# Sliding-window attention and a SiLU feed-forward: batch 1's q and k turned two positions at once, a margin on landings in the planned order, shorter fillers, one weight piece moved

## The chip, the cores and the metric

The kernel runs on one core of one Trainium2 chip. A core has five engines that run side by side: TensorE (PE; its weight loads are shown apart as PEld), VectorE (DVE), ScalarE (ACT), GpSimd (POOL) and SyncE (SP). POOL and SP also issue DMAs. The metric is the device time of one execution in microseconds (us); lower is better. A kernel's time is the median of several runs.

## What is computed

Eight batches of eight heads, 576 positions, head size 64. Each position attends to itself and the 63 before it. The result, 4608 rows of 512, goes through a feed-forward layer with SiLU.

```python
scores = scale * np.matmul(q, k.transpose(0, 1, 3, 2))
mask = (rel >= 0) & (rel < 64)
scores = np.where(mask, scores, -1000000000.0)
attn = softmax(scores)
x = np.matmul(attn, v)  # [8, 8, 576, 64] to [4608, 512]
h = x @ w_in            # [512, 2048]
out = (h * sigmoid(h)) @ w_out   # [2048, 512]
```

## The kernel before

**Order.** Nothing is scheduled by the framework. A class `Plan` writes the order by hand: every piece of work is put in with the engines that may do it, a cost in us, what it depends on, and a rank. `Plan.run` then plays a clock forward in a small model of its own. Whenever an engine is free it takes the ready piece of lowest rank, and in the end the pieces are emitted in that order. On the chip each engine goes through its list in order and waits at an instruction whose inputs are not there, with all that stands behind it. The model's times are thus only used to choose the order. For a DMA, `op["seen"]` is when the model believes that it has landed.

**Loads.** q, k, v, w_in and w_out come in through POOL's queue, cast to bf16 on the way. Only the first q and k go through SP. POOL issues in this order: q1, k1, then the constants `ident` and `window` (memsets and selects on POOL itself), then q2, q3, k2, k3 and the four v parts of batch 0 (`FIRST_LOADS`), eight pieces of w_in, and batch 1. Batch 1 has a q and a k load for each of four head pairs `pj` (here called positions) into the tiles `natb`, with v parts 0 and 1 after pair 1 and parts 2 and 3 after pair 3. Then come eight pieces of w_out, and batch 2.

**Turns.** q and k are needed with the head dimension on the partitions, so `natb` is turned on TensorE by a matmul with the identity `ident`, into a PSUM bank. `natb` holds 96 partitions with six positions side by side for each of two heads. `turn_heads` takes one position of one head at a time: 12 matmuls for a pair (line 315), then one copy, `lift` (line 340), into `qt` or `kt`. `turn_twos` takes two positions of a head side by side: 6 matmuls (line 324). The even positions then lie on partitions 0 to 63 and the odd ones on 64 to 127, and four copies, `lift_twos` (line 333), carry out one head and one parity each. Before, batch 1's q and k use `turn_heads`, the q of batches 2 and 3 use `turn_twos`, and the rest is transposed by DMA (line 268). Batch 0 has a form of its own (`turn_first`, line 303).

**Attention.** A batch has three groups of three 64-position blocks. For batches 0 and 1 a group is two units, one for pairs 0 and 1 and one for 2 and 3. A unit is: scores (line 365), exp on ACT (379), mask on DVE (382), values (388), reciprocal and scaling on DVE (395, 401), a turn back on PE (405) and the copy into `bridge` (416).

**Feed-forward.** Nine tiles of 512 rows. First layer: 16 groups of four matmuls of 512 columns (line 421), each followed by SiLU on ACT (427). Second layer: 64 matmuls (line 430), copied out and stored by SP. Tile 0's first layer runs while batch 1 is loaded and turned; its second layer shares TensorE with batch 1's attention. Tile 1's first layer needs all of batch 1's `bridge`.

**PSUM.** Eight banks: four called `at` (turns and scores) and four called `mp` (feed-forward, values of later batches).

**Fillers.** Up to 60 matmuls of `ident` (line 685, class "warm", lowest rank) are put in wherever TensorE would stand idle in the model, until the first feed-forward matmul is placed.

Of the kernel before, what the change touches and what calls it, by code (L numbers as in the profile page):

```python
# [14 lines left out]
class Plan:  # L15
# [35 lines left out]
    def run(self):  # L51
# [7 lines left out]
        while left:  # L59
# [6 lines left out]
            while moved:  # L66
                moved = False
                for e in engines:
                    if free[e] > now:
                        continue  # L70
                    best, kept = None, set()
                    heads = [(self.queues[c][head[c]], c) for c in can[e] if head[c] < len(self.queues[c])]
                    for op, c in sorted(heads, key=lambda x: x[0]["first"]):
                        if e == "POOL" and op["dma"] and len(sent) >= 8 and sent[-8] > now:
                            continue
                        if e not in op["us"] or not self.done(op["deps"]) or (op["gate"] and not op["gate"]()):
                            continue
# [12 lines left out]
                        break  # L90
                    if best is None:
                        continue
                    op, c = best
                    head[c] += 1
                    us = op["us"][e]
                    if op["table"] and op["table"] != table:
                        table, us = op["table"], us + 1.28
                    end = free[e] = now + us
                    soft = e == "POOL"
                    if op["dma"] is None:  # L100
                        op["seen"] = end + op["lat"]
# [25 lines left out]
def kernel(ctx, tc, q, k, v, w_in, w_out, out):  # L127
    nc = tc.nc
# [165 lines left out]
    def at_bf16(op, i=0):  # L294
        return banks[op["bank"][i]].bitcast(BF16)[:, 0:S]
# [10 lines left out]
                        is_transpose=True, start=(m == 0), stop=(m == NM0 - 1),  # L306
                    )

    def turn_heads(op, w):

        pst = at_bf16(op).rearrange("x (m p) -> x m p", m=NM)
        heads = natbs[w][0:NR].rearrange("p (h m d) -> p h m d", h=2, m=NM)
        for m in range(NM):
            for hh in range(2):
                nc.tensor.matmul(
                    pst[64 * hh:64 * hh + 64, m], lhsT=heads[:, hh, m], rhs=ident[0:NR, 0:NR],
                    is_transpose=True, start=(m == 0), stop=(m == NM - 1),
                )

    def turn_twos(op, w):  # L320

        pst = at_bf16(op).rearrange("x (m p) -> x m p", m=NM)
# [6 lines left out]
    def place_one(b, pj, kk):  # L329
        return kt[b % NK][:, 64 + pj * S:64 + (pj + 1) * S] if kk else qt[b % NK][:, pj * S:(pj + 1) * S]  # L330

    def lift_twos(e, op, b, pj, hh, r):
        copies[e](  # L333
            out=place_one(b, pj, 0)[64 * hh:64 * hh + 64].rearrange("x (p m) -> x p m", m=NM)[:, :, r::2],
            in_=at_bf16(op)[64 * r:64 * r + 64].rearrange("x (h m p) -> x h p m", h=2, m=NM // 2)[:, hh],
        )

    def lift(e, op, b, pj, kk, i=0):
        m = NM if b else NM0
        copies[e](  # L340
            out=place_one(b, pj, kk).rearrange("x (p m) -> x p m", m=m),
            in_=at_bf16(op, i).rearrange("x (m p) -> x p m", m=m),
        )

    def shift_v(e, b, hf, a, z):
# [119 lines left out]
    def late(b):  # L465
        return hold.get(b)

    def add_first_batch():
        got = {}
        for what, u in FIRST_LOADS:  # L470
# [21 lines left out]
            for i in range(2):  # L492
                x = 2 * a + i
                tu["untils"][i].append(p.add("lift", {"ACT": 0.64, "DVE": 0.75}, lambda e, tu=tu, x=x, kk=kk, i=i:
                                             lift(e, tu, 0, x, kk, i), [tu, c_k[0]]))
                kq_done[(0, x)] = kq_done.get((0, x), []) + tu["untils"][i]
            for w in ws:
                natb_free[w] = tu

    def add_batch_qk(b):  # L500
        pool = "at" if b else "all"
        slot, parts = {}, {0: [], 1: []}
        for pj in range(NP):
            kq_done[(b, pj)] = []
        for pj in range(NP):
            busy = s_last.get((b - NK, pj), []) + ([c_k[b % NK]] if b < NK else [])
            for kk in range(2):
                if b >= (NXK if kk else NXQ):
                    if pj % 2 == 0:
# [1 line left out]
                        n_nat[0] += 1  # L511
                    i = slot[kk]
                    parts[kk] += [p.add("dma", {"POOL": 0.72}, lambda _, i=i, pj=pj, kk=kk, hh=hh: load_rows(i, b, pj, kk, hh),
                                        [nat_free.get(i)], dma=0.5, gate=late(b)) for hh in range(2)]
# [7 lines left out]
                    for x in (pj - 1, pj):  # L522
# [2 lines left out]
                w = n_nat[1] % NNB  # L525
                n_nat[1] += 1
                ca = [p.add("dma", {"POOL": 0.66}, lambda _, w=w, pj=pj, kk=kk: load_cast(w, b, pj, kk),
                            [natb_free.get(w)], dma=0.65, gate=late(b))]
                twos = b > 1 and not kk
                tu = p.add("turn", {"PE": 0.27 if twos else 0.5}, None, ca + [c_ident], lat=0.1, pool=pool, b=b)  # L530
                tu["fn"] = lambda _, tu=tu, w=w, twos=twos: (turn_twos if twos else turn_heads)(tu, w)
                li = []
                if twos:
                    for hh, r in [(0, 0), (0, 1), (1, 0), (1, 1)]:
                        li.append(p.add("lift", {"ACT": 0.48, "DVE": 0.48}, lambda e, tu=tu, pj=pj, hh=hh, r=r:
                                        lift_twos(e, tu, b, pj, hh, r), [tu] + busy + li, b=b))
                else:
                    li.append(p.add("lift", {"ACT": 0.64, "DVE": 0.75}, lambda e, tu=tu, pj=pj, kk=kk:
                                    lift(e, tu, b, pj, kk), [tu] + busy, b=b))
                tu["untils"][0] = li  # L540
                natb_free[w] = tu
                kq_done[(b, pj)] += li
            if b < NIV and pj % 2:
                add_v_loads(b, [pj - 1, pj], [c_vv[b]])

    def add_v_loads(b, parts, busy):
        v_landed.setdefault(b, []).extend(
            p.add("dma", {"POOL": 1.0}, lambda e, part=part: load_v(e, b, part), busy, dma=1.1, gate=late(b)) for part in parts)

    def add_batch_v(b):  # L550
        busy = pv_last.get(b - NV, []) + [c_vv[b % NV]]
# [189 lines left out]
```

## Time and profile before

| what | us |
|---|---|
| median of 7 runs | 310.39 (308.93 to 315.34) |
| the profiled execution | 308.93, span 307.2 |
| PE busy, whole span | 296.6 |
| first matmul of the feed-forward (line 421) starts | 19.83 |
| batch 1's turns (line 315) | 26.36 to 34.28 |
| first second-layer matmul (line 430) | 39.38 |
| tile 1's first layer starts | 59.55 |
| POOL's last loads are issued | about 160 |

The span in 40 slices (7.7 us each; busy tenths):

```profile
PE   5999999999999999999999999999999999999995
DVE  2671447433653057304650266005500000000000
ACT  4887777678548665667456745773574146216611
POOL 8957759869697586852860000000000000000000
DMA  7999999999999999999999949303310110010011
```

A digit 9 means 90% or more. TensorE is full from the second slice on; the DMA engines are full for the first 60% of the span, while the inputs come in. The time from a load's issue to its landing is read from its semaphore: the landings named in this document are those times in the trace.

### The profile page before, as it was taken

The page shows a single profiled execution, that of the slowest core. Times are in us where ns is not written, and L with a number is a line of the kernel's source. Part 1 is how long each engine was busy: PE and PEld are TensorE (multiplying, and loading weights), DVE is VectorE, ACT ScalarE, POOL GpSimd, SP SyncE. Part 2 cuts the span into 40 slices and gives each one's busy share as a digit, 9 for nine tenths or more (in the row PEclk, how much of TensorE's full clock was granted, in tenths as well). Part 3 has the DMA queues.
Part 4 walks back from the last instruction along what each step waited for, and adds up shares of the span by engine and source line. Part 5 has one row for each costly group of instructions (what it writes and reads, how often), then busy time and mean ns, then how long its engine had stood idle before and what let it go on. Part 6 is the DMA issues. An engine that isn't in the chain of part 4 may idle for free.

```text
span 307.2 us, 6690 instructions
## 1 busy us (share of the span) xinstructions
PE 296.6 (97%) x2704; PEld 148.1 (48%) x2733; DVE 93.8 (31%) x256; ACT 180.4 (59%) x331; POOL 118.6 (39%) x159
## 2 busy tenths in 40 slices
PE   5999999999999999999999999999999999999995
PEld 3575445444554445445544454444544444444444
DVE  2671447433653057304650266005500000000000
ACT  4887777678548665667456745773574146216611
POOL 8957759869697586852860000000000000000000
PEclk9999999999999999999999999999999999999999
DMA  7999999999999999999999949303310110010011
GB/s 156 172 196 184 184 199 161 126 236 173 161 175 149 156 162 162 175 166 138 195 147 176 109 128 198 69 2 93 98 25 2 68 68 1 36 68 34 2 68 68
DMA packets 137598, 37.56 MB, mean 122 GB/s; under 512 B 122464, under 2 KB 132832, under 8 KB 137568
## 3 DMA queue, kind: packets, MB, share of 16 engines
q0 software_dynamic: 95328, 18.06, 76.0%
q1 hardware_dynamic: 42240, 19.08, 32.9%
q8 instruction: 21, 0.34, 0.4%
q14 instruction: 9, 0.07, 0.1%
HBM read 36.70 MB, written 9.44 MB: 150 GB/s over the span
## 4 chain that ended last, share of the span: by engine, by line
PE 87%; DMA 6%; POOL 5%; issue 2%; ACT 0%; POOLq 0%; ACTq 0%
PE mp L430 41%; PE mp L421 38%; DMA w_in_sb<-in_moe_w_in_dram 4%; PE at L365 3%; PE mp L388 3%; DMA natb<-in_k_dram 2%; POOL w_in_sb L282 2%; POOL vv L276 1%; POOL natb L249 1%; PE at L324 1%; PE at L388 1%; PE at L405 0%; POOL natb L243 0%; PE mp L405 0%; ACT g L427 0%
## 5 line engine op out<-in xcount | busy, mean ns | idle before, releaser
L430 PE MATMUL mp<-w_out_sb,g 128*128 128x512 bf16 (+2 forms) x579 | 128.7, 368 | 2.9 <-issue 2.1
L421 PE MATMUL mp<-bridge,w_in_sb 128*128 128x512 bf16 (+2 forms) x600 | 129.6, 370 | 0.2 <-ACT g L427 0.2
L427 ACT ACTIVATE g<-mp 128x512 bf16<-128x512 f32 (+2 forms) x150 | 85.6, 580 | 32.4 <-PE mp L421 31.6
L421 PEld LDWEIGHTS <-w_in_sb 128*128 128x128 bf16 x600 | 57.4, 97 | 66.7 <-issue 6.3
L430 PEld LDWEIGHTS <-g 128*128 128x128 bf16 x608 | 55.6, 98 | 58.5 <-issue 0.2
L379 ACT ACTIVATE e<-at 128x384 bf16<-128x384 f32 x90 | 37.8, 497 | 23.1 <-PE at L365 22.7
L436 ACT COPY ot<-mp 128x512 f32<-128x512 f32 (+2 forms) x31 | 17.2, 558 | 57.4 <-PE mp L430 39.5
L262 POOL DMA_DIRECT2D nat<-in_k_dram x48 | 35.9, 753 | 19.5 <-DMA vv<-in_v_dram 10.1
L382 DVE TENSOR_TENSOR e<-e,mask 128x384 bf16<-128x384 bf16 x84 | 27.0, 352 | 46.4 <-ACT e L379 45.8
L276 POOL DMA_DIRECT2D vv<-in_v_dram x32 | 32.4, 1022 | 6.5 <-PE mp L421 2.3
L262 POOL DMA_DIRECT2D nat<-in_q_dram x32 | 24.3, 767 | 6.3 <-DMA nat<-in_q_dram 3.7
L401 DVE TENSOR_TENSOR ox<-mp,rc 128x384 bf16<-128x384 f32 x39 | 19.3, 534 | 0.0
L388 PEld LDWEIGHTS <-e 128*64 128x64 bf16 x576 | 11.5, 110 | 10.9 <-issue 9.5
L395 DVE RECIPROCAL rc<-mp 128x6 f32<-128x6 f32 x39 | 7.3, 192 | 21.7 <-PE mp L388 21.7
L365 PEld LDWEIGHTS <-kt 64*128 64x128 bf16 x576 | 10.0, 95 | 6.3 <-issue 5.5
L365 PE MATMUL at<-qt,kt 64*128 64x64 bf16 x540 | 12.4, 191 | 0.0
L436 DVE COPY ot<-mp 128x512 f32<-128x512 f32 x7 | 4.7, 690 | 24.0 <-PE mp L430 23.7
L333 DVE COPY qt<-at 64x288 bf16<-64x288 bf16 x18 | 8.6, 479 | 8.8 <-ACT qt L333 5.6
L388 PE MATMUL mp<-vv,e 128*64 128x65 bf16 x468 | 11.2, 196 | 0.0
L350 DVE COPY vv<-vv 64x576 bf16<-64x576 bf16 (+1 forms) x13 | 7.7, 592 | 7.1 <-issue 3.6
L243 POOL DMA_DIRECT2D natb<-in_q_dram x12 | 7.9, 655 | 4.5 <-DMA w_out_sb<-in_moe_w_out_dram 1.1
L348 DVE COPY vv<-vv 64x576 bf16<-64x576 bf16 (+1 forms) x13 | 8.5, 651 | 0.2
(63 smaller groups left out, 123.7 us busy)
## 6 DMA issues: line engine op xcount, KB each, us to landing
out_dram<-ot SPq DMA_DIRECT2D x35, 256.0 KB, 2.6
vv<-in_v_dram POOLq DMA_DIRECT2D x32, 144.0 KB, 7.0
nat<-in_k_dram POOLq DMA_DIRECT2D x48, 72.0 KB, 7.5
nat<-in_q_dram POOLq DMA_DIRECT2D x32, 72.0 KB, 7.9
natb<-in_q_dram POOLq DMA_DIRECT2D x15, 144.0 KB, 6.7
w_in_sb<-in_moe_w_in_dram POOLq DMA_DIRECT2D x8, 256.0 KB, 8.0
w_out_sb<-in_moe_w_out_dram POOLq DMA_DIRECT2D x8, 256.0 KB, 7.4
natb<-in_k_dram POOLq DMA_DIRECT2D x7, 144.0 KB, 5.9
```

What stands on the lines that cost most here:

```text
L262: nc.gpsimd.dma_start(out=rows(i)[:, pj % 2, :, 64 * hh:64 * hh + 64], in_=(q, k)[kk][b, head(pj, hh)].rearrange("(m p) d -> p m d", p=NR),)
L276: queue[e].dma_start(out=vv[b % NV][:, 2 * g0 + 1:2 * g1 + 1:2, 0:D], in_=v[b].rearrange("h s d -> (h s) d").rearrange("(g p) d -> p g d", ...
L333: copies[e](out=place_one(b, pj, 0)[64 * hh:64 * hh + 64].rearrange("x (p m) -> x p m", m=NM)[:, :, r::2], in_=at_bf16(op)[64 * r:64 * r + ...
L365: nc.tensor.matmul(at_six(of[hh])[:, j, x], lhsT=kt[b % NK][r, at:at + 128], rhs=qt[b % NK][r, at:at + 64], start=(b > 0 and j == x == 0), ...
L379: nc.scalar.activation(out=es[n % NE], in_=at_six(bank), func=ACTF.Exp, scale=scale)
L382: nc.vector.tensor_mul(es[n % NE], es[n % NE], mask0 if g == 0 else mask)
L388: nc.tensor.matmul(at_pv(bank)[64 * hh:64 * hh + 64, j, x], lhsT=es[(2 * n + hh) % NE][:, j, x], rhs=vv[b % NV][:, head(2 * a + j, hh) * N ...
L401: nc.vector.tensor_mul(ox(n), at_pv(bank)[:, :, :, 0:D], rcs[n % NRC].unsqueeze(3).to_broadcast([128, 2, 3, D]))
L421: nc.tensor.matmul(banks[bank["bank"][0]][:, lo:hi], lhsT=w_in_sb[:, c, ft * 128:(ft + 1) * 128], rhs=bridge[:, (j * TT + lo) // 64:(j * T ...
L427: nc.scalar.activation(out=gts[gt][:, lo:hi], in_=banks[bank["bank"][0]][:, lo:hi], func=ACTF.Silu)
L430: nc.tensor.matmul(banks[bank["bank"][0]][:, 0:hi - lo], lhsT=gts[gt][:, m * 128:(m + 1) * 128], rhs=w_out_sb[:, f, lo:hi], start=(f == 0) ...
L436: copies[e](out=ots[ot][:, lo:hi], in_=banks[bank["bank"][0]][:, 0:hi - lo])
```

## The change

It does five things.

1. Batch 1's q and k are turned by `turn_twos` and carried out by four `lift_twos` each, to `qt` or `kt`. `turn_heads` goes, and `lift` stays for batch 0 alone.
2. In the model, the loads of later q and k, of v from batch 1 on, and of w_out count as landed 1.3 us later (`MARGIN`). The kernel on the chip has no wait for that; only the order can change.
3. Fillers end when the last exp of batch 0 is placed, not when the first feed-forward matmul is.
4. w_out's first piece (`EARLY_OUT`) is issued ahead of batch 1's v parts 2 and 3, not behind them.
5. q2 and q3 of batch 0 join q1 and k1 in the class "early", whose rank is ahead of the constants on POOL. The q turns of batch 3 take `mp` banks instead of `at`.

```diff
-                        op["seen"] = pipe[True] + (1.2 if now < 40 else 3.2)
+                        op["seen"] = pipe[True] + op["lat"] + (1.2 if now < 40 else 3.2)
...
-    FIRST = 6
+    FIRST, EARLY_OUT = 6, 1
...
-    NM0, LEAD = 9, 1.5
+    NM0, LEAD, MARGIN = 9, 1.5, 1.3
...
-    def lift_twos(e, op, b, pj, hh, r):
+    def lift_twos(e, op, b, pj, kk, hh, r):
         copies[e](
-            out=place_one(b, pj, 0)[64 * hh:64 * hh + 64].rearrange("x (p m) -> x p m", m=NM)[:, :, r::2],
+            out=place_one(b, pj, kk)[64 * hh:64 * hh + 64].rearrange("x (p m) -> x p m", m=NM)[:, :, r::2],
...
-                ca = p.add("early" if u == 1 else "dma", {"POOL": 0.6}, lambda _, w=w, u=u, kk=kk: load_first_cast(w, u, kk), dma=0.8)
+                ca = p.add("early" if (what, u) in FIRST_LOADS[2:6] else "dma", {"POOL": 0.6}, lambda _, w=w, u=u, kk=kk: load_first_cast(w, u, kk), dma=0.8)
...
+    def add_w_out(which):
+        wout.extend(p.add("dma", {"POOL": 0.75}, lambda _, f=f: load_w_out(f), dma=1.29, lat=MARGIN) for f in which)
+
     def add_batch_qk(b):
-        pool = "at" if b else "all"
+        pool = "mp" if b == 3 else "at"
...
-                            [natb_free.get(w)], dma=0.65, gate=late(b))]
-                twos = b > 1 and not kk
-                tu = p.add("turn", {"PE": 0.27 if twos else 0.5}, None, ca + [c_ident], lat=0.1, pool=pool, b=b)
-                tu["fn"] = lambda _, tu=tu, w=w, twos=twos: (turn_twos if twos else turn_heads)(tu, w)
+                            [natb_free.get(w)], dma=0.65, gate=late(b), lat=MARGIN)]
+                tu = p.add("turn", {"PE": 0.27}, None, ca + [c_ident], lat=0.1, pool=pool, b=b)
+                tu["fn"] = lambda _, tu=tu, w=w: turn_twos(tu, w)
                 li = []
-                if twos:
-                    for hh, r in [(0, 0), (0, 1), (1, 0), (1, 1)]:
...
-                else:
-                    li.append(p.add("lift", {"ACT": 0.64, "DVE": 0.75}, lambda e, tu=tu, pj=pj, kk=kk:
-                                    lift(e, tu, b, pj, kk), [tu] + busy, b=b))
+                for hh, r in [(0, 0), (0, 1), (1, 0), (1, 1)]:
+                    li.append(p.add("lift", {"ACT": 0.48, "DVE": 0.48}, lambda e, tu=tu, pj=pj, kk=kk, hh=hh, r=r:
+                                    lift_twos(e, tu, b, pj, kk, hh, r), [tu] + busy + li, b=b))
...
             if b < NIV and pj % 2:
+                if pj == 3:
+                    add_w_out(range(EARLY_OUT))
                 add_v_loads(b, [pj - 1, pj], [c_vv[b]])
...
-    p.add_filler(60, "warm", {"PE": 0.26}, warm, [c_ident], gate=lambda: moe[0][0]["seen"] is None,
+    p.add_filler(60, "warm", {"PE": 0.26}, warm, [c_ident], gate=lambda: exps[0][-1]["seen"] is None,
...
-            for f in range(8):
-                wout.append(p.add("dma", {"POOL": 0.8}, lambda _, f=f: load_w_out(f), dma=1.28))
+            add_w_out(range(EARLY_OUT, 8))
```

The row loads of k and q (`load_rows`) and the v loads from batch 1 on get `lat=MARGIN` in the same way. On each queue the new order is: POOL issues q1, k1, q2, q3, the constants, k2, k3, v and so on as before, and further down w_out piece 0 between batch 1's pair 3 and its v part 2. SP's queue is not edited.

More of the change, by code (lines that the diff above doesn't have):

```diff
@@ L307, in turn_first @@
                     )
[L309 to L318, printed above, removed]
     def turn_twos(op, w):
@@ L330, in place_one, with lift @@
         return kt[b % NK][:, 64 + pj * S:64 + (pj + 1) * S] if kk else qt[b % NK][:, pj * S:(pj + 1) * S]
-    def lift_twos(e, op, b, pj, hh, r):
+    def lift_twos(e, op, b, pj, kk, hh, r):
         copies[e](
-            out=place_one(b, pj, 0)[64 * hh:64 * hh + 64].rearrange("x (p m) -> x p m", m=NM)[:, :, r::2],
+            out=place_one(b, pj, kk)[64 * hh:64 * hh + 64].rearrange("x (p m) -> x p m", m=NM)[:, :, r::2],
             in_=at_bf16(op)[64 * r:64 * r + 64].rearrange("x (h m p) -> x h p m", h=2, m=NM // 2)[:, hh],
         )
-    def lift(e, op, b, pj, kk, i=0):
-        m = NM if b else NM0
+    def lift(e, op, pj, kk, i):
         copies[e](
-            out=place_one(b, pj, kk).rearrange("x (p m) -> x p m", m=m),
-            in_=at_bf16(op, i).rearrange("x (m p) -> x p m", m=m),
+            out=place_one(0, pj, kk).rearrange("x (p m) -> x p m", m=NM0),
+            in_=at_bf16(op, i).rearrange("x (m p) -> x p m", m=NM0),
         )
@@ L494, in add_first_batch @@
                 tu["untils"][i].append(p.add("lift", {"ACT": 0.64, "DVE": 0.75}, lambda e, tu=tu, x=x, kk=kk, i=i:
-                                             lift(e, tu, 0, x, kk, i), [tu, c_k[0]]))
+                                             lift(e, tu, x, kk, i), [tu, c_k[0]]))
                 kq_done[(0, x)] = kq_done.get((0, x), []) + tu["untils"][i]
@@ L513, in add_batch_qk @@
                     parts[kk] += [p.add("dma", {"POOL": 0.72}, lambda _, i=i, pj=pj, kk=kk, hh=hh: load_rows(i, b, pj, kk, hh),
-                                        [nat_free.get(i)], dma=0.5, gate=late(b)) for hh in range(2)]
+                                        [nat_free.get(i)], dma=0.5, gate=late(b), lat=MARGIN) for hh in range(2)]
                     if pj % 2 == 0:
@@ L527, in add_batch_qk @@
                 ca = [p.add("dma", {"POOL": 0.66}, lambda _, w=w, pj=pj, kk=kk: load_cast(w, b, pj, kk),
-                            [natb_free.get(w)], dma=0.65, gate=late(b))]
-                twos = b > 1 and not kk
-                tu = p.add("turn", {"PE": 0.27 if twos else 0.5}, None, ca + [c_ident], lat=0.1, pool=pool, b=b)
-                tu["fn"] = lambda _, tu=tu, w=w, twos=twos: (turn_twos if twos else turn_heads)(tu, w)
+                            [natb_free.get(w)], dma=0.65, gate=late(b), lat=MARGIN)]
+                tu = p.add("turn", {"PE": 0.27}, None, ca + [c_ident], lat=0.1, pool=pool, b=b)
+                tu["fn"] = lambda _, tu=tu, w=w: turn_twos(tu, w)
                 li = []
-                if twos:
-                    for hh, r in [(0, 0), (0, 1), (1, 0), (1, 1)]:
-                        li.append(p.add("lift", {"ACT": 0.48, "DVE": 0.48}, lambda e, tu=tu, pj=pj, hh=hh, r=r:
-                                        lift_twos(e, tu, b, pj, hh, r), [tu] + busy + li, b=b))
-                else:
-                    li.append(p.add("lift", {"ACT": 0.64, "DVE": 0.75}, lambda e, tu=tu, pj=pj, kk=kk:
-                                    lift(e, tu, b, pj, kk), [tu] + busy, b=b))
+                for hh, r in [(0, 0), (0, 1), (1, 0), (1, 1)]:
+                    li.append(p.add("lift", {"ACT": 0.48, "DVE": 0.48}, lambda e, tu=tu, pj=pj, kk=kk, hh=hh, r=r:
+                                    lift_twos(e, tu, b, pj, kk, hh, r), [tu] + busy + li, b=b))
                 tu["untils"][0] = li
@@ L547, in add_v_loads @@
         v_landed.setdefault(b, []).extend(
-            p.add("dma", {"POOL": 1.0}, lambda e, part=part: load_v(e, b, part), busy, dma=1.1, gate=late(b)) for part in parts)
+            p.add("dma", {"POOL": 1.0}, lambda e, part=part: load_v(e, b, part), busy, dma=1.1, gate=late(b), lat=MARGIN * (b > 0)) for part in parts)
     def add_batch_v(b):
```

## The prediction

> **What bounds the kernel now.** I read the page's busy times and chain first, then the chain in order of time, then TensorE's timeline where that chain leaves TensorE.
>
> ```profile
> PE 296.6 (97%) x2704; PEld 148.1 (48%) x2733; DVE 93.8 (31%) x256; ACT 180.4 (59%) x331; POOL 118.6 (39%) x159
> ...
> PE 87%; DMA 6%; POOL 5%; issue 2%; ACT 0%; POOLq 0%; ACTq 0%
> ```
>
> PE carries 87% of the chain. The rest is loading at the start, up to 33.9 us, as the chain in order of time shows (start, length, what):
>
> ```profile
> 27.66 6.20 DMA natb<-in_k_dram
> 33.90 0.45 PE at L315 x12
> 34.35 4.64 PE mp L421 x21
> ...
> 54.77 4.75 PE mp L430 x22
> 59.55 5.99 PE mp L421 x27
> ```
>
> The last k load of batch 1 lands at 27.66 + 6.20 = 33.86, and its turn starts at 33.90. From there PE runs to the end (304.1) with nearly no gap: between 38.9 and 59.5 it is busy 20.39 of 20.60 us. So a microsecond of PE time or PE wait saved ahead of 39 us is one off the end, if nothing behind runs late. TensorE's timeline (start, length to the modelled end, line):
>
> ```profile
> 28.27 0.39 PE L421 MATMUL mp<-bridge,w_in_sb 128*128 128x512 bf16 x1
> 28.92 0.45 PE L315 MATMUL at<-ident,natb 96*64 96x96 bf16 x12 [0.26 <-DMA natb<-in_k_dram]
> ...
> 31.77 0.45 PE L315 MATMUL at<-ident,natb 96*64 96x96 bf16 x12
> 32.15 0.39 PE L421 MATMUL mp<-bridge,w_in_sb 128*128 128x512 bf16 x1
> 32.47 0.45 PE L315 MATMUL at<-ident,natb 96*64 96x96 bf16 x12
> ...
> 33.90 0.45 PE L315 MATMUL at<-ident,natb 96*64 96x96 bf16 x12 [0.29 <-DMA natb<-in_k_dram]
> 34.28 4.71 PE L421 MATMUL mp<-bridge,w_in_sb 128*128 128x512 bf16 x21
> ```
>
> Each turn stands in PE's order just where its load lands, and where the load is late, the first-layer matmuls behind it wait too. Batches 2 and 3 already turn q two positions at once:
>
> ```profile
> 65.37 0.42 PE L324 MATMUL at<-ident,natb 96*128 96x96 bf16 x6
> 65.63 1.68 PE L421 MATMUL mp<-bridge,w_in_sb 128*128 128x512 bf16 x7
> 67.14 0.42 PE L324 MATMUL at<-ident,natb 96*128 96x96 bf16 x6
> ```
>
> **The turns.** Between 65.63 and 67.14 seven matmuls take 1.51 us, 0.216 each. A two-position turn then adds 65.63 - 65.37 = 0.26 us. A one-position turn adds 32.15 - 31.77 = 0.38, plus a slower entry: from 32.15 the next turn follows after 0.32, 0.104 over a matmul's 0.216. That is 0.48 us. The stretch from the last matmul ahead of the first turn (26.05) to 34.28 is 8.23 us and holds 16 matmuls (3.46), so eight turns and their waits cost 4.77. Eight turns at 0.48 are 3.86, the waits 0.91. With turns at 0.26 (2.08) and no wait, 4.77 - 2.08 = 2.69 us go: 1.78 from the form, 0.91 from the waits.
>
> A rule speaks against the first part. The Trainium skill, "TensorE: Matmul & The Clock Gate", section on LDWEIGHTS, says that a weight load takes the number of its columns over 1.2 GHz. By that, 12 loads of 64 columns and 6 of 128 cost the same (an estimate: 0.64 us both), and the form would save nothing; the sum would be 1.78 us smaller. The rows disagree: 109 ns for a load of 64 columns at L315, 98 for 128 at L324. I go by the rows.
>
> **The margin.** With 1.3 us added to planned landings, turns stand later in PE's order, behind about six more 0.216 us matmuls. The lateness seen was under 0.4 us a time (0.652 from matmul to turn at 28.92, against 0.32). Once PE has gained some 2.7 us against the loads, though, a turn would meet its load that much earlier, and the margin gives back only part: I keep 0.2 us of wait (bounds 0 and 0.91). After 59.5 the margin only shifts turns and scores among matmuls; I take nothing (bounds: a gain of 0.2, the idle time left between 38.9 and 59.5, and a loss of 0.5, about one more wait like today's largest). On POOL the loads keep their order, and SP's queue is not touched.
>
> **The lifts, the price of the form.** A turn was carried out of PSUM by one copy and now takes four, each waiting for the one before in the same tile (duration min/median/max):
>
> ```profile
> L340 ACT COPY kt<-at x3: 638/638/639, 27.6 to 33.0; 128x576 bf16<-128x576 bf16 x3
> L340 DVE COPY kt<-at x1: 758/758/758, 34.5 to 34.5; 128x576 bf16<-128x576 bf16 x1
> ...
> L333 DVE COPY qt<-at x18: 467/480/491, 49.1 to 74.4; 64x288 bf16<-64x288 bf16 x18
> L333 ACT COPY qt<-at x14: 466/474/479, 50.4 to 75.3; 64x288 bf16<-64x288 bf16 x14
> ```
>
> Before: 6 x 0.64 + 2 x 0.76 = 5.4 us. After: 32 x 0.48 = 15.4 us, so 10 us more for ACT and DVE. Here is what they have (length; busy us of PE, PEld, DVE, ACT, POOL):
>
> ```profile
> 26.30:38.90 12.60, 11.88 (x133) 5.83 (x132) 4.29 (x10) 9.11 (x15) 10.44 (x15) 1.00 1.64 182
> ```
>
> Free are 8.3 us of DVE and 3.5 of ACT: 11.8 for 10 more. It fits barely, and half of it comes late: the last four loads land from 31.7 to 33.9. Sixteen lifts of batch 2 took 7.7 us on both engines (49.09 to 56.82) beside attention work; from 32.2 that ends at 39.9. Batch 1's first scores need only positions 0 and 1 and can start at 38.9 - 2.7 = 36.2. The second unit needs 2 and 3; it started at 39.1, now about 40. In between PE has second-layer matmuls. The attention's last bridge then ends at 54.4 + 0.9 = 55.3, and tile 1's first layer, which needs it, starts at 59.55 - 2.7 = 56.85: covered by 1.5 us. I take 0.4 us of loss (bounds 0, and 1 us if the order places those scores before the lifts are out). A lift on ACT between two silus (busy 0.60 of each 0.87 us) delays a silu by 0.2 us; four `mp` banks, 3.5 us of matmuls, cover that.
>
> **w_out ahead of v.** w_out's first piece is issued at 28.28 in place of v part 2 and lands one piece's pace after 33.86: 1.34 (two pieces land at 38.39 and 39.73), so 35.2 instead of 36.97. It is needed by the first L430, at 36.2 + 0.45 = 36.65: without the move PE would wait 0.3. The second piece lands at 38.39 as now, and PE reaches it after eight matmuls, 36.65 + 1.73 = 38.38: level. v parts 2 and 3 land at 36.1 and 37.1 instead of 34.78 and 35.80; their DVE shifts wait, and behind them the values of unit 2, later than that anyway. Nothing, then.
>
> **q2 and q3 early.** Two issues (3.74 to 4.88, 1.14 us) move ahead of `ident` and `window` on POOL. `ident` is done at 4.2 instead of 3.05; the first turn needs it at 5.14, when ACT's cast is in. The fillers start 1.14 us later. DVE's bias waits as long, needed only at 8.8. The loads land at 6.03 (k1), then 7.90, 8.60, 9.35, 10.17: a hole of 1.1 us closes, but k2 is issued as late as now and the fastest load took 4.0 us, so what follows gains some 0.4. Batch 0's end hangs on DVE, gapless from 13.1 to 20.6, which starts on v: 0.3 us gained (bounds: 0.4, and a loss of 0.5 if late fillers slow the first turns).
>
> **Fillers end sooner.** Four run from 19.17 to 19.83 ahead of the first L421. But its input is ready only when DVE's second bridge ends, 19.11 + 0.55 = 19.66. So 0.1 us at most. **Batch 3's turns in `mp`**: a bank held some 2.7 us (65.37 to 68.07) leaves three for first-layer groups whose own round is about 1.8 us. Nothing (bounds 0 and a loss of 0.3).
>
> **Sum**: 2.69 - 0.2 - 0.4 + 0.3 + 0.1 = 2.5 us. The profiled run took 308.93 (span 307.2): 306.4. It was the fastest of the seven; the median, 310.39, lies 1.46 above, so I say 310.4 - 2.5 = 307.9. The bounds: all good 2.69 + 0.2 + 0.4 + 0.1 = 3.4, so 307.0; all bad 2.69 - 0.91 - 0.5 - 1.0 - 0.5 - 0.3 = -0.5, so 310.9.
>
> **Rivals.** *The lifts eat it.* With 10 us more ACT and DVE are 23.4 of 25.2 us taken in that stretch, so scores and silus run late and 1.5 to 2.5 us of the gain go: 309.4 to 310.4, no change. For it: that share, 93%. Against: DVE's 4.29 of 12.6 us today.
>
> *The attention of batch 1 runs out of cover (slower).* Tile 1's first layer waits once unit 2's scores start after 39.1 + (56.85 - 54.4) = 41.5. If the last sixteen lifts run on one engine at the chained pace of batch 2's first turn (DVE starts 49.09 and 49.84, 0.75 apart), they end at 34.2 + 16 x 0.75 = 46.2: 4.7 us lost against 2.7 won, 312.4. For it: the chain of four, and ACT's silus come first. Against: two chains interleave and ACT took 14 of 32 such copies.
>
> *The clock.* Fillers start at 4.24. Full rate came after 8 us: 36 turn matmuls take 0.99 us at 5.14 and 0.66 at 10.22. If it comes some 3.4 us later (5.14 to 8.6 again), at most half of that is lost, 1.7: 309.6. The Trainium skill, same page, Part 1, has the full clock follow a busy, free-running window of 3.4 us; by it a start 1.1 us later costs a whole window in about a third of the runs (an estimate). One profile cannot show it.
>
> *Only the form works*, the margin moving nothing useful: 1.8 - 0.4 + 0.4 = 1.8, 308.6. It lies inside the forecast.
>
> **Chances.** Forecast with the last case, 0.65, own range 306.4 to 308.8; lifts 0.15; clock 0.05; cover 0.15. About 0.5% (1.55 us) is what can be told from no change: faster (under 308.8) 0.65, same 0.20, slower (over 311.9) 0.15. The range reaches up through both middle cases to the edge of the slower one: 306.2 to 311.6.
>
> **What would show it.** Right: eight groups of six L324 matmuls ahead of the first L430 with no DMA releaser, the first L430 near 36.7, tile 1's first L421 near 56.9, w_out's first landing near 35. Wrong: PE waiting at L365 for DVE or ACT `kt` or `qt` near 40, at L421 for a bridge near 57, or turns of 0.99 us past 8.6.

## The result: 313.39 us, slower by 0.7%, and the profile after

The changed kernel takes 313.39 us (median of 27 runs, 309.64 to 316.89); the kernel before, on the same chips, 310.35 (64 runs, 308.49 to 315.62). The ratio is 1.0073, with a 95% interval of 1.0052 to 1.0094; it compares the fast runs alone, those within 1.5% of the fastest of their kernel, while the medians of all runs are 1.0% apart. The forecast was 307.9. The profiled execution after took 314.84 us, 1.4 above the median, span 313.1.

The steps of both profiled executions, each time the start of the first matmul of that kind (us):

| step | before | after | difference |
|---|---|---|---|
| tile 0, first layer | 19.8 | 20.0 | +0.2 |
| tile 0, second layer | 39.4 | 36.6 | -2.8 |
| tile 1, first layer | 59.5 | 59.0 | -0.5 |
| tile 2 | 92.2 | 93.3 | +1.1 |
| tile 3 | 124.7 | 125.5 | +0.7 |
| tile 4 | 156.9 | 163.5 | +6.6 |
| tile 5 | 189.1 | 194.6 | +5.5 |
| end of TensorE | 304.0 | 309.6 | +5.6 |

At 36.6 TensorE is 2.8 us ahead, but 0.7 of that is work that no longer stands ahead of this point and comes behind it. At tile 1, 0.5 is left. Then tile 3 lasts 38.0 us in place of 32.2. On the page, the lines that answer to those shown of before are the busy times, the chain and, of the 40 slices, the granted clock (before, all 40 digits are 9):

```profile
PE 296.2 (95%) x2645; PEld 147.5 (47%) x2675; DVE 102.7 (33%) x273; ACT 184.9 (59%) x340; POOL 117.5 (38%) x159
...
PEclk9999999999999999999799999999999999999999
...
PE 79%; DMA 13%; POOL 3%; issue 2%; DVE 1%; ACT 0%; SPq 0%; POOLq 0%; ACTq 0%
```

TensorE does no more work than before, but carries 79% of the chain, not 87, and DMA carries 13%. One slice, the twentieth (149 to 157 us), has a clock below full. The chain in order of time says which DMA (start, length, what):

```profile
125.64 12.23 PE mp L409 x56
...
138.36 10.66 DMA kt<-nat
149.58 4.44 PE mp L418 x12
```

At 138.36 SP issues the transpose of batch 5's last two k pairs; it lands 10.66 us later. TensorE's timeline (line 353 is the scores, 376 the values, 418 the second layer, in the changed kernel's numbers):

```profile
144.72 0.35 PE L353 MATMUL at<-qt,kt 64*128 64x64 bf16 x12
149.07 0.35 PE L353 MATMUL at<-qt,kt 64*128 64x64 bf16 x12 [4.00 <-DMA kt<-nat]
149.58 4.44 PE L418 MATMUL mp<-w_out_sb,g 128*128 128x512 bf16 x12 [0.16 <-issue]
```

The first half of batch 5's first unit runs, the second half waits 4.0 us for `kt`, and the twelve matmuls behind take 4.44 us, 0.37 each. The stretches around it (length; busy us of PE, PEld, DVE, ACT, POOL; granted clock; DMA share; GB/s) show why:

```profile
145.10:149.00 3.90, 0.00 (x0) 0.00 (x0) 1.39 (x4) 0.87 (x2) 1.02 (x2) 1.00 1.90 108
149.86:153.27 3.41, 3.41 (x10) 1.19 (x9) 0.72 (x2) 0.46 (x2) 2.25 (x4) 0.50 1.81 187
```

After 3.9 us without a matmul the clock is granted at half for 3.41 us; that is some 1.7 us of matmuls lost. Wait and clock together, 4.0 + 1.7, are the 5.8 us by which tile 3 is longer.

The times of the other executions fit this. One such half-clock stretch takes the mean granted clock of a whole execution to 0.995 (0.5 x 3.41 us of 313.1 lost), and 23 of the 28 executions of the changed kernel have 0.995 or less, with a median of 313.82 us. The five without took 309.64 to 312.00, with a median of 310.19, no slower than the kernel before.

Before, the same `kt` was issued at 136.04, landed at 146.25, and was needed at 147.8:

```profile
147.84 0.52 PE L365 MATMUL at<-qt,kt 64*128 64x64 bf16 x24
```

So it comes 2.8 us later after, but is also needed 3 us sooner; together they use up the 1.6 us to spare. Of the 2.8, 2.3 are a later issue. On SP's queue the transposes and the store ahead of this one follow one another with almost no gap, from 122.78 before and from 123.63 after, and they take 1.5 us longer in all after; why is not shown. Why it is needed sooner is seen in tile 1's second layer (matmuls of the scores between 70 and 90 us, 24 to a unit), before and after:

```profile
L365 PE MATMUL at<-qt,kt x72: 190/190/200, 76.5 to 87.3; 64*128 64x64 bf16 x72
```

```profile
L353 PE MATMUL at<-qt,kt x96: 190/190/200, 73.5 to 87.2; 64*128 64x64 bf16 x96
```

Three units of attention before, four after: from there all attention runs one unit ahead. Batch 5's first unit is the third to start in tile 3's second layer before (138.8, 144.0, 147.8), the second after (139.6, 144.7).

How the front part went. The turns and lifts of the changed kernel (line 313 is the turn of two positions, 409 the first layer, 322 the four lifts):

```profile
28.19 0.42 PE L313 MATMUL at<-ident,natb 96*128 96x96 bf16 x6
28.45 0.60 PE L409 MATMUL mp<-bridge,w_in_sb 128*128 128x512 bf16 x2
28.88 0.42 PE L313 MATMUL at<-ident,natb 96*128 96x96 bf16 x6
...
36.64 2.09 PE L418 MATMUL mp<-w_out_sb,g 128*128 128x512 bf16 x7
38.66 0.35 PE L353 MATMUL at<-qt,kt 64*128 64x64 bf16 x12
38.94 0.82 PE L418 MATMUL mp<-w_out_sb,g 128*128 128x512 bf16 x3
40.74 0.41 PE L313 MATMUL at<-ident,natb 96*128 96x96 bf16 x6 [0.98 <-DVE kt L322]
```

```profile
L322 DVE COPY kt<-at x10: 471/478/487, 29.7 to 42.3; 64x288 bf16<-64x288 bf16 x10
...
L322 ACT COPY kt<-at x6: 471/475/479, 31.3 to 43.8; 64x288 bf16<-64x288 bf16 x6
```

Each turn adds 0.26 us (28.45 - 28.19), as forecast, and none waits for its load. But seven, not eight, stand ahead of the second layer. The eighth is at 40.74 and waits 1.0 us for a lift: a bank is free only when four lifts are out, and the last of these copies starts at 43.8.

### The profile page after: what moved, and what is told of

The parts are those of the page before. It is cut to its first block, busy times and chain, and to the rows that moved or that the text cites. A ratio compares the mean times of both kernels' runs of the same rounds, so it can differ in the third digit from the quotient of the medians.

```text
span 313.1 us, 6586 instructions
## 1 busy us (share of the span) xinstructions
PE 296.2 (95%) x2645; PEld 147.5 (47%) x2675; DVE 102.7 (33%) x273; ACT 184.9 (59%) x340; POOL 117.5 (38%) x159
## 4 chain that ended last, share of the span: by engine, by line
PE 79%; DMA 13%; POOL 3%; issue 2%; DVE 1%; ACT 0%; SPq 0%; POOLq 0%; ACTq 0%
PE mp L418 37%; PE mp L409 35%; DMA kt<-nat 3%; DMA natb<-in_q_dram 3%; PE mp L376 3%; DMA w_out_sb<-in_moe_w_out_dram 3%; PE at L353 3%; DMA vv<-in_v_dram 2%; DMA nat<-in_k_dram 1%; POOL natb L249 1%; POOL w_out_sb L288 1%; POOL vv L276 1%; PE at L376 1%; POOL natb L243 0%; PE at L313 0%
## 5 line engine op out<-in xcount | busy, mean ns | idle before, releaser
L418 PE MATMUL mp<-w_out_sb,g 128*128 128x512 bf16 (+2 forms) x578 | 131.5, 371 | 2.9 <-issue 1.9
L418 PEld LDWEIGHTS <-g 128*128 128x128 bf16 x608 | 55.7, 98 | 59.0 <-issue 2.5
L367 ACT ACTIVATE e<-at 128x384 bf16<-128x384 f32 x88 | 36.8, 497 | 26.3 <-PE at L353 25.2
L424 ACT COPY ot<-mp 128x512 f32<-128x512 f32 (+2 forms) x28 | 15.4, 555 | 57.5 <-PE mp L418 44.9
L262 POOL DMA_DIRECT2D nat<-in_k_dram x48 | 35.2, 738 | 17.3 <-DMA nat<-in_k_dram 7.6
L262 POOL DMA_DIRECT2D nat<-in_q_dram x32 | 23.6, 741 | 14.1 <-DMA nat<-in_q_dram 6.5
L389 DVE TENSOR_TENSOR ox<-mp,rc 128x384 bf16<-128x384 f32 x37 | 18.5, 537 | 0.0
L383 DVE RECIPROCAL rc<-mp 128x6 f32<-128x6 f32 x37 | 7.1, 195 | 20.6 <-PE mp L376 20.5
L424 DVE COPY ot<-mp 128x512 f32<-128x512 f32 x10 | 6.8, 690 | 20.0 <-PE mp L418 18.9
L338 DVE COPY vv<-vv 64x576 bf16<-64x576 bf16 (+1 forms) x14 | 8.7, 624 | 5.9 <-DMA vv<-in_v_dram 5.6
L322 DVE COPY qt<-at 64x288 bf16<-64x288 bf16 x16 | 7.7, 479 | 7.5 <-ACT qt L322 7.1
## 6 DMA issues: line engine op xcount, KB each, us to landing
vv<-in_v_dram POOLq DMA_DIRECT2D x32, 144.0 KB, 8.2
natb<-in_q_dram POOLq DMA_DIRECT2D x15, 144.0 KB, 6.3
natb<-in_k_dram POOLq DMA_DIRECT2D x7, 144.0 KB, 5.5
```

What stands on the lines that cost most here:

```text
L262: nc.gpsimd.dma_start(out=rows(i)[:, pj % 2, :, 64 * hh:64 * hh + 64], in_=(q, k)[kk][b, head(pj, hh)].rearrange("(m p) d -> p m d", p=NR),)
L338: copies[e](out=t[64:128, 0:-1:2], in_=t[0:64, 1::2])
L367: nc.scalar.activation(out=es[n % NE], in_=at_six(bank), func=ACTF.Exp, scale=scale)
L389: nc.vector.tensor_mul(ox(n), at_pv(bank)[:, :, :, 0:D], rcs[n % NRC].unsqueeze(3).to_broadcast([128, 2, 3, D]))
L418: nc.tensor.matmul(banks[bank["bank"][0]][:, 0:hi - lo], lhsT=gts[gt][:, m * 128:(m + 1) * 128], rhs=w_out_sb[:, f, lo:hi], start=(f == 0) ...
L424: copies[e](out=ots[ot][:, lo:hi], in_=banks[bank["bank"][0]][:, 0:hi - lo])
```

## The experiments

Fifteen runs followed, of thirteen kernels (h1 and h2 repeat f1 and g1); each ratio is against runs of the kernel before on the same chip, beside the kernel. Three theories stood at the start. U: the attention is one unit ahead, and batch 5's `kt` comes after its scores. L: the four lifts and the banks they hold cost the time in the first 60 us. D: batch 5's k is late in any case.

**e1, the extra unit sent back.** Batch 3's first unit may not run ahead of tile 2's second layer:

```diff
+    tile_at = {}
...
+        tile_at[j] = len(moe)
...
-                  ... gate=lambda: scores_may_run(whole), ...
+                  ... gate=lambda: scores_may_run(whole) and (b != 3 or scores_may_run.i >= tile_at.get(2, 10 ** 9)), ...
```

> The changed kernel, with one gate more in the order: batch 3's first unit of attention may not be placed ahead of tile 2's second layer. The emitted order is untouched up to there. In the changed kernel four whole units stand in tile 1's second layer where the kernel before has three, so all later attention runs one unit ahead, and batch 5's first scores wait 4.0 us at 145 us for a k transpose that lands at 149.0. Theory U (one unit ahead of the loads): that wait and the half clock after it, 5.8 us of tile 3, go, and the time is 308 to 309.5 against 310.35 before (ratio 0.993 to 0.998). Rival L (the four lifts and their banks in the first 60 us are the loss): nothing in the first 60 us is touched, so 312.5 to 314, ratio 1.005 to 1.01. Rival D (batch 5's k simply comes late, whatever the order of the units): the scores of batch 5 still wait 2 us or more near 146, 311.5 to 313.5.

Measured: 310.04, ratio 0.9991 (0.9958 to 1.0025).

**e2, batch 3's turns back in `at`.**

```diff
-        pool = "mp" if b == 3 else "at"
+        pool = "at"
```

> The changed kernel with batch 3's q turns back in the banks called at; all else as changed. The order then has three units in tile 1's second layer again, by another way than a gate. U: no wait over 1 us for kt near 146, 308 to 309.5. L: 312.5 to 314, as nothing ahead of 60 us differs. D: a wait of 2 us or more stays, 311.5 to 313.5.

Measured: 310.03, ratio 0.9994 (0.9971 to 1.0017); three units in tile 1 again.

**e3, no margin.**

```diff
-    NM0, LEAD, MARGIN = 9, 1.5, 1.3
+    NM0, LEAD, MARGIN = 9, 1.5, 0.0
```

> The changed kernel with a margin of 0 in place of 1.3 us. The order has three units in tile 1's second layer, and the turns of batch 1 stand 1.3 us earlier in it. U: no wait over 1 us for kt near 146; but turns meet their loads, with waits of 0.3 to 1 us in all between 26 and 36: 308.5 to 310.5. L: the lifts are as many as in the changed kernel, so 312.5 to 314. D: 311.5 to 313.5.

Measured: 309.76, ratio 0.9998 (0.9981 to 1.0014); three units.

**e4, batch 1 by one position and one lift**, as before the change, with the other four edits:

```diff
-                tu["fn"] = lambda _, tu=tu, w=w: turn_twos(tu, w)
+                twos = b > 1
...
+                tu["fn"] = lambda _, tu=tu, w=w, twos=twos: (turn_twos if twos else turn_heads)(tu, w)
...
```

> The changed kernel with batch 1 turned one position at a time again (12 matmuls and one lift a turn), all else as changed. The order still has four units in tile 1's second layer. U: a wait for kt between 140 and 150 stays (1 to 5 us), and the turns cost 1.8 us more, while the first 60 us lose the waits at lifts: 312 to 315. L: lifts gone, so the time falls to that of the kernel before or under, 309 to 310.5. D: 312 to 314.

Measured: 313.96, ratio 1.0141 (1.0126 to 1.0156); four units stay. What TensorE waits for in e4 (total, times, longest us):

```profile
PE at L365 <- DMA kt<-nat: 3.6, 2, 2.7
```

The four point one way. Wherever tile 1 has three units the loss is gone, and it needs both the margin and the `mp` banks to make four (e2, e3). Without the lifts, but with four units, it stays (e4). L and D fall as causes of the loss; U stands.

**e5 and e6: where is the gain of the turns?** All of e1 to e3 merely equal the kernel before, where U had e1 and e2 at 308 to 309.5, although the first L430 (L418 by the changed numbers) starts at 36.0 to 37.6 in them. On top of e2, e5 turns only batch 1's q by two positions, e6 neither q nor k. M: the form's gain is given back before tile 1. F: it is worth 1.8 us at the end.

```diff
+                twos = b > 1 or not kk    # e5
+                twos = b > 1              # e6
```

> On the version with batch 3's turns back in the banks called at (310.03 against 309.92 before, so level): of batch 1 only q is turned two positions at once, k one at a time again. 16 + 4 lifts in place of 32, four turns dearer by 0.22 us, 0.9 us in all. Theory M (the form gives 1.8 us ahead of the first second-layer matmul, and what it gives is lost at lifts, w_out's pieces and a late turn before tile 1 starts): tile 0's second layer is 1 to 1.5 us shorter than the 22.2 us of that version, tile 1's first layer starts within 0.5 us of its 58.2, ratio to the kernel before 0.997 to 1.001. Rival F (the form is worth its 1.8 us at the end, the loss lies elsewhere): 0.9 us slower than that version, ratio 1.001 to 1.004.

> On the same version: batch 1 is turned one position at a time throughout, so that of the change only the margin, the early loads, the earlier w_out piece and the shorter fillers stay. M: tile 0's first layer is 1.8 us longer and its second layer 2 us shorter (about 20.2), so the end moves by under 0.5 us: ratio 0.998 to 1.002. F: 1.8 us slower: ratio 1.004 to 1.008.

Measured: e5 309.89, ratio 0.9995 (0.9961 to 1.0029); e6 309.81, ratio 0.9993 (0.9959 to 1.0026). With three units the form is worth nothing that can be told. Tile 1 starts at 58.2 in e2, 57.6 in e5, 58.6 in e6.

**e7 and e8: a second limit.** In e2 the first layer of tile 3 waits for the transpose of batch 3's second group into `bridge`, which lands at 124.04. e7 turns the last group of batch 2 and the first two of batch 3 back on TensorE, e8 has six `nat` buffers for eight, so that fewer loads run beside the transposes:

```diff
-    NXQ, NXK, NXO = 4, 2, 3
+    NXQ, NXK, NXO = 4, 2, 4           # e7
-    NN, NNB, NE, NOT, NGT = 8, 8, 12, 4, NFT + 3
+    NN, NNB, NE, NOT, NGT = 6, 8, 12, 4, NFT + 3    # e8
```

> On the same version: the attention results of batch 2's last and batch 3's first two groups go to the bridge by TensorE turns and copies and not by DMA transposes. That adds 36 matmuls, about 1.0 us of TensorE, and takes three transposes off SP's queue. Theory P (a second limit: bridge transposes land at 124 to 126 us just when tile 3's first layer wants them, so whatever PE gains ahead of it is spent there): the wait of 0.6 us for the bridge at tile 3 goes, tile 3 starts 0.5 to 1.2 us sooner than 124.2, and batch 5's first scores have over 2 us to spare; ratio 0.996 to 1.000. Without a second limit: 1.0 us slower, ratio 1.002 to 1.005.

> On the same version: six buffers for the row loads and not eight, so that loads of later batches are held back on POOL and share the DMA engines less with the transposes that are wanted sooner; the planned order of TensorE is the same. Theory C (the transposes take 8 to 10 us because loads for batches 6 and 7 run beside them): the bridge at tile 3 and batch 5's k land 1 to 3 us sooner, the wait at tile 3 goes, ratio 0.995 to 0.999. Rival S (the transposes are slow by themselves, or SP's queue is what they wait in): landings as before, and the loads held back come late: ratio 1.000 to 1.02.

Measured: e7 309.69, ratio 0.9995 (0.9979 to 1.0011); e8 309.75, ratio 0.9993 (0.9977 to 1.0009). In e7 the wait is gone and 1.0 us of turns takes its place (three groups, 0.33 each). In e8 batch 5's `kt` lands at 136.83 (e2: 146.67), but the bridge at 124.96, no sooner, and TensorE waits for it:

```profile
122.93 0.82 PE L418 MATMUL mp<-w_out_sb,g 128*128 128x512 bf16 x3
125.10 3.18 PE L409 MATMUL mp<-bridge,w_in_sb 128*128 128x512 bf16 x14 [1.35 <-DMA bridge<-ox]
```

So six buffers help `kt` and not the bridge. That gave the reverse test.

**f1, the changed kernel with six buffers and nothing else.** Its order on TensorE is the changed kernel's, four units included. f2 is e5 with six buffers, f3 is f2 with e7's edit.

> The changed kernel with nothing altered but six nat buffers in place of eight, so that the loads of later k rows are issued in another spacing; TensorE's order is the changed kernel's, four units of attention in tile 1's second layer. In the run with fewer nat buffers and the shift undone, batch 5's kt landed at 136.8. Theory U (the attention one unit ahead is dear only because batch 5's kt comes after its scores): the scores of batch 5, needed near 144.9, wait for nothing, the half clock behind the wait goes too, tile 3's stage is back from 38.0 us to 32 to 33, and the time is 309.0 to 310.5. Rival (the order itself, with four units in one second layer, is what costs, whatever lands when): tile 3 still lasts 36 us or more, or another stage grows by as much, and the time stays 312 to 314.

> The changed kernel with batch 3's turns in at, only the q of batch 1 by two positions, and six nat buffers. If the limits that the earlier runs showed (tile 0's second layer, batch 5's kt) are all there is, 309.0, 0.4% under before; if the bridge transpose at tile 3 is a limit that sets in whatever comes earlier, 309.7, no change: the transpose lands at 124 to 125 and the first layer of tile 3 starts then.

> As the run before, and batch 3's second group turned back on TensorE, so that tile 3 needs no bridge transpose. If that transpose is the last limit, tile 3's first layer starts near 122.5 to 123.5 and, less about 1 us of added turns on TensorE, the time is 308.8 to 309.3. If what is won ahead of tile 3 is given back as in the earlier runs, 309.7, no change.

Measured: f1 308.40, ratio 0.9943 (0.9921 to 0.9964); f2 309.11, ratio 0.9967 (0.9942 to 0.9991); f3 309.31, ratio 0.9976 (0.9957 to 0.9995). f1 is 5.0 us under the changed kernel's median, 4.0 by the ratios, which allow for the chips. Its `kt` is issued at 133.10, not 138.36, and lands at 139.71, ahead of the scores at 144.4; tile 3 lasts 32.2 us. SP's queue (start, us on the queue), of the changed kernel and then of f1:

```profile
134.70 3.44 SPq L268 DMA_TRANSPOSE qt<-nat  x1
138.36 2.65 SPq L268 DMA_TRANSPOSE kt<-nat  x1
```

```profile
131.61 1.28 SPq L268 DMA_TRANSPOSE qt<-nat  x1
133.10 1.54 SPq L268 DMA_TRANSPOSE kt<-nat  x1
```

U passes the reverse test: the order is no loss once the load is there. It is even the better order: e8, with six buffers too but three units, stays at 0.9993. f2, with three units, still waits for the bridge (1.7 us, to 124.94); f3, where that group is turned back on TensorE, starts tile 3 at 123.5 and is no faster; f1 does not wait, since batch 3's second unit ran one place sooner.

**g1, the control: the kernel before with six buffers.**

> The kernel before with six nat buffers in place of eight and nothing else, the control for the changed kernel with six, which took 308.4. Theory U with the gain from the change: before, batch 5's kt was already in time, so six buffers alone bring nothing, 310.0 to 310.6, and the 1.9 us belong to the five edits. Rival (the 1.9 us belong to the buffers): 308.2 to 309.0 here as well, and the five edits bring nothing even with batch 5's kt in time. Half and half: 309.3.

Measured: 309.36, ratio 0.9965 (0.9931 to 0.9999). That lies half way, and it was another chip. Of the 17 executions of the kernel before beside it, 7 had a mean clock of 0.995 or less; the other ten have a median of 309.58, so against these the buffers bring 0.2 us. Both ran once more, side by side on one chip (h1, h2), with h3, which is e4 with six buffers.

> The changed kernel with six nat buffers, once more, beside the kernel before with six on the same chip. If the five edits gain by themselves once batch 5's kt is in time, 308.2 to 308.7 here and 309.2 to 309.8 there, a ratio of about 0.997 between them. If the difference between the earlier two came from their chips, the two agree within 0.4.

> The kernel before with six nat buffers, on the same chip as the run ahead: 309.2 to 309.8 if the five edits gain 1 us of their own, 308.4 to 308.8 if they gain nothing.

> The changed kernel with six nat buffers and all of batch 1's q and k by one position and one lift each; the other four edits and the four units in tile 1's second layer stay. If the form of the turns carries the gain (forecast 1.8 us, seen by itself less than 0.5), 309.2 to 310.0. If the gain comes from the attention being one unit ahead, with batch 5's kt in time, 308.2 to 308.8. Batch 5's kt lands near 140 and no stall of over 1 us stands at its scores in either case.

| kernel with six buffers | median us | ratio to before, interval |
|---|---|---|
| h1, all five edits | 307.96 (6 runs) | 0.9914 (0.9886 to 0.9941) |
| h2, the kernel before | 310.06 (12 runs) | 0.9989 (0.9968 to 1.0009) |
| h3, four edits, batch 1 by one position | 309.68 (12 runs) | 0.9981 (0.9957 to 1.0005) |

With `kt` in time the five edits are worth 310.06 - 307.96 = 2.1 us on this chip, and 309.68 - 307.96 = 1.7 of it is the form of the turns. The earlier pair, f1 and g1 on two chips, gives 1.0 us (0.7 by the ratios), so the size is less sure than the sign. In h3 `kt` landed at 143.90 and not near 140, still ahead of its scores at 145.1. Where the time is, in the stretches from tile 0's first layer to the start of tile 3 (columns as above), for h1 and then h3:

```profile
19.70:36.20 16.50, 16.37 (x138) 10.33 (x137) 8.37 (x19) 14.21 (x31) 11.89 (x17) 1.00 1.63 186
36.20:58.30 22.10, 21.25 (x257) 10.85 (x256) 15.91 (x43) 16.56 (x35) 17.64 (x25) 1.00 1.74 176
58.30:92.70 34.40, 34.32 (x357) 17.16 (x357) 21.26 (x51) 25.32 (x49) 26.91 (x34) 1.00 1.94 178
92.70:124.80 32.10, 32.10 (x321) 15.48 (x321) 13.08 (x39) 19.46 (x36) 18.82 (x25) 1.00 1.90 157
```

```profile
19.70:38.30 18.60, 18.47 (x217) 11.12 (x216) 7.32 (x16) 14.21 (x30) 13.86 (x19) 1.00 1.57 190
38.30:58.50 20.20, 20.10 (x228) 10.26 (x227) 10.78 (x31) 14.57 (x32) 14.91 (x20) 1.00 1.83 153
58.50:93.00 34.50, 33.91 (x332) 16.86 (x332) 20.56 (x48) 23.17 (x45) 26.12 (x33) 1.00 2.02 178
93.00:125.80 32.80, 32.78 (x344) 15.87 (x344) 13.52 (x40) 19.72 (x37) 20.37 (x27) 1.00 2.12 155
```

Both start the first layer at 19.7. The first stage is 2.1 us shorter in h1, but a unit's scores and the eighth turn have only moved into the next, which is 1.9 longer: stage by stage the gain seems to come and go. The sums tell more. Over the four stretches h1 has 1073 matmuls and h3 1121: the 48 that eight turns of six save against eight of twelve, and nothing else. Busy time is 104.0 against 105.3 us, so the form saves 1.2 us of TensorE; at the end h1 is 1.3 ahead in the profiles (303.05 against 304.32) and 1.7 in the medians. Against h2 the bridge counts too, at least in the execution that was profiled: it took 311.23, 1.2 above its median, and g1's profile of the same kernel has no such wait. What TensorE waits for in h2, where the transpose lands at 126.88 and tile 3 starts at 127.0:

```profile
PE mp L421 <- DMA bridge<-ox: 1.8, 1, 1.8
```

In h1 it landed at 120.51, and tile 3 started at 124.8 with no wait.

## Why the prediction was wrong

**Right:** the front of the kernel, in the main. First second-layer matmul near 36.7: it was 36.64, but in part by luck. The forecast had all eight turns and batch 1's first scores ahead of it; measured, seven turns and no scores stood there. With the eighth turn (0.26) and the scores (0.46) it would have been 37.4, so 2.0 us were won at equal work and not 2.7. w_out's first piece near 35: 34.98. No turn waited for its load. The turns' form at 1.78 us: 1.7 between the medians of h1 and h3, 1.3 in their profiles. The sum of 2.5 us: 2.1 with `kt` in time between h2 and h1, 1.0 between g1 and f1. The rule weighed against the form, in the Trainium skill, "TensorE: Matmul & The Clock Gate", section on LDWEIGHTS (columns over 1.2 GHz, so no gain from 6 loads of 128 columns for 12 of 64), does not hold here: a load of 64 columns lasted 109 ns, where the rule gives 53 (an estimate), and one of 128 lasted 97; a turn of six adds 0.26 us, as forecast.

**The step that failed** is the one on the margin, "After 59.5 the margin only shifts turns and scores among matmuls; I take nothing", with a loss of 0.5 as its bound, and beside it "Batch 3's turns in `mp`": "Nothing". Together they put a fourth unit into tile 1's second layer, and that is not a shift among matmuls: it moves every later unit one place forward against loads whose times did not move forward (batch 5's `kt` even landed 2.8 us later). In the profiled execution it cost 4.0 us of wait and 1.7 of half clock. e1 undoes that alone, e2 and e3 one each of the two edits that make it, and all three come to 309.8 to 310.0; f1 leaves it and brings the load forward, and comes to 308.4.

**The premise that was not followed to the end** is "a microsecond of PE time or PE wait saved ahead of 39 us is one off the end, if nothing behind runs late". The condition was looked at up to 59.5 us only. The trace of before held both deadlines behind it: batch 3's bridge landed at 124.59 and tile 3 began at 124.7; batch 5's `kt` landed at 146.25 and was needed at 147.8. If these landings stay, a kernel that runs 2.5 us sooner up to there meets the first with 2.4 us missing and the second with 0.9. SP's timeline of before has both transposes (start, us on the queue, line; the first line is two of batch 3's, its second group's and the one behind it, the last is batch 5's second `kt`); the page's lists by busy time show neither, since a landing is no busy time:

```profile
116.83 5.11 SPq L410 DMA_TRANSPOSE bridge<-ox  x2
...
136.04 3.00 SPq L268 DMA_TRANSPOSE kt<-nat  x1
```

From 116.83 to the landing at 124.59 is 7.8 us, from 136.04 to 146.25 is 10.2. In e2, where tile 2 began 1.2 us sooner than before, the two were 7.8 and 10.0: a sooner TensorE did not shorten them. The bridge, which takes the attention's results, landed 0.55 us sooner (124.04), and `kt` 0.4 later (146.67).

**Mis-sized terms.** *The lifts*, 0.4 us: tile 0's second layer took 22.36 us after, 20.17 before. Of these 2.2 us, 0.72 is work that before stood ahead of that layer (a unit's scores, 0.46, and the eighth turn, 0.26); some 1.5 is waiting, 1.0 of it the eighth turn at a bank held for four lifts. The cover of 1.5 us was there for the attention, but the turn itself stood in the way. Up to tile 1 this was the rival "the lifts eat it": 0.5 us was left. *w_out, second piece level*: 0.8 us of wait in e2, where TensorE came 0.6 us sooner than after; none after. *q2 and q3 early*, 0.3 us gained: not seen. The first first-layer matmul starts at 18.7 to 20.5 us in the fourteen profiles with the edit, 19.7 in the middle, against 19.8, 19.8 and 20.1 in the three without.

**The rivals.** *The attention of batch 1 runs out of cover*, 312.4, comes near in size and is wrong in place: no wait for a bridge of batch 1 decides anything at 59.0. The right kind of rival would have been a late transfer behind a shifted order, and it was not among them. *The clock* at the start: full rate came at 9.9 us after, 8.6 before, and the first L421 0.2 us later.

**Open.** That the two deadlines also make up the spread of the kernel before (308.49 to 315.62) is not shown. It fits their slack of 0.1 and 1.6 us, and it fits the clock: of the 128 executions of that kernel beside the experiments, 23 have a mean clock of 0.995 or less, all but one at 311.7 to 315.7 us, and none of the others is above 312.3. But only one execution of it was profiled, near the lowest of its times. Why SP issued batch 5's `kt` later in the changed kernel stays open too. What the margin alone wins at the turns was not tried with `kt` in time.

## What to carry to other kernels

Before a microsecond saved early is counted at the end, list every later transfer that TensorE meets with less slack than the saving, with its landing and the start of its user; those are the next bounds, and here there were two. In an order that a planner writes, a change in believed landing times or buffers can move whole units of work between stages: look where each unit stands, not only at the place that was edited. When a change that should gain loses, bring the late transfer forward and leave the order alone: here that turned a loss of 0.7% into a gain of 0.6 to 0.9%, with one number changed that gives the kernel before 0.1 to 0.35%.

## What the runs showed of the hardware

**A wait near 4 us costs a second time.** After 3.9 us without a matmul the clock fell to 0.50 for 3.41 us. In e4's profiled execution a wait of 2.7 us (146.28 to 148.97) left it at full; two of its three others have a mean clock of 0.995, so this wait too may be longer at times. The Trainium skill, "TensorE: Matmul & The Clock Gate", Part 1, has an idle window of about 3.4 us bring the half rate and a busy one of the same length end it; both profiles agree.

**A transpose's time in flight was anything from 4 to 11 us.** The same transpose of batch 5's `kt`, issue to landing: 10.66 us after, 10.2 before, 6.6 in f1 and 4.05 in e8. On SP's queue the two issues shown took 6.1 us after and 2.8 in f1. With six buffers POOL has to hold back loads of later batches, and in f1 waits 8.4 us between 110 and 160 for a `qt` transpose to free one; after has no such wait. That `kt` lands sooner for want of those loads is the likely reading, not one that was tried apart. For the bridges near 116 us, which land 7.8 us after issue in before and e2, 8.5 in e8 and 9.6 in h2, six buffers brought nothing.
